# A gated linear attention with a feed-forward layer on one core: work by head and sequence, or by slabs of 128 tokens and 8 heads

## The chip, the core and the metric

The kernel runs on one core of a Trainium2 chip. A core has TensorE (PE, matrix products into PSUM; its weight loads are the row PEld), VectorE (DVE), ScalarE (ACT, functions from tables that are loaded as sets), GpSimd (POOL) and SyncE (SP, which here only issues DMAs); 16 DMA engines move data between DRAM and on-chip memory. Each engine works through its own list of instructions in order, and waits at an instruction until what it needs is there. The metric is the time of one execution on the device, in microseconds (us).

## The reference

The first stage is a linear attention with a complex gate for every token and channel: a state S of 48 x 48 for each of 4 x 8 heads is multiplied by the gate, takes up k v, and is read by q, over 768 tokens. The second is a gated feed-forward layer over all 3072 tokens.

```python
# B, H, S, D = 4, 8, 768, 48; d_model 384, d_ff 1536
mag = np.sqrt(a_re * a_re + a_im * a_im)
scale = np.minimum(mag, 0.999) / (mag + 1e-06)
a_re_n, a_im_n = (a_re * scale, a_im * scale)
for t in range(S):
    new_re = ar * S_re - ai * S_im
    new_im = ar * S_im + ai * S_re
    kv = np.einsum('bhd,bhe->bhde', k[:, :, t], v[:, :, t])
    S_re, S_im = (new_re + kv, new_im)
    y[:, :, t] = np.einsum('bhd,bhde->bhe', q[:, :, t], S_re)
x = y.transpose(0, 2, 1, 3).reshape(B * S, H * D)
gate = 1.0 / (1.0 + np.exp(-(x @ w_gate)))
out = gate * (x @ w_val) @ w_out
```

## The kernel before

The sequence is cut into 6 chunks of 128 tokens. A product of gates is a sum of log magnitudes and a sum of phases, and inside a chunk both sums are one product with a triangular matrix: `cl_ps` (L183) for the logs, `ct_ps` (L196) for the phases, both fp32. With exp of half the log sum and sine and cosine of the phase sum, q and k become rotated vectors `qst` and `kst`, 112 wide per head: 48 cosine parts, 16 zeros, 48 sine parts. Inside a chunk, attention is then k-transposed-q scores times a triangular mask, times v.

The outer loop runs over the 4 batches. `emit_prep(b)` loads q, k, v, a_re and a_im of one batch, head by head, as 128 x 288 tiles (128 tokens of each of 6 chunks), squares the gate (L149, L151), clips it (L153), divides im by re through a reciprocal (L159, L160), and takes Ln (L163) and Arctan (L165). The batch's loop then makes, for every head, `ee` = exp (L185, L186), the phase wrap (L200 to L206: round on ScalarE, subtract, then fold for the cosine on VectorE), sine and cosine (L209, L211) and the rotated vectors (L227 to L233).

Because sums are taken within a chunk and centred, going from chunk to chunk multiplies the state by a complex number per channel. Rows of `ee` and `cs` go to DRAM (`scr`) and back as columns (`rbe`, `rbc`, `rbn`), from which `alr` and `ngi` are formed (L245 to L264); the state's real part lies on partitions 0 to 47 and its imaginary part on 64 to 111, and L308 to L335 update it with operations on 48 partitions.

The chunk loop works by pairs of heads: four transposes (L282, L283) of the rotated vectors, one copy `qkT` (L286), two score products (L288), one mask (L290), then per head the output `py` (L297, L300), which has 48 rows and 128 token columns, its eviction `xall` (L302), and the state's new part `pkv` (L304). DMAs copy `xall` into `xt`, whose 128-partition tiles cross head borders. `emit_moe` then does 384 tokens at a time: 12 blocks of gate `pg` (L102), value `pv` (L107), tanh (L112) and product `p` (L114), and three output blocks `po` (L120). It uses two PSUM buffers. The order on each engine is set by a scheduler from the program order; POOL issues the loads of v and of the weights, SP all other DMAs.

## Time and profile before

| | us |
|---|---|
| median of 3 runs (624.09 to 624.98) | 624.13 |
| span of the profiled execution | 622.0 |
| DVE busy | 418.3 |
| PE busy | 384.9 |
| ACT busy | 304.7 |
| POOL busy | 275.5 |

Busy time is the sum of an engine's instructions; PE's are pipelined, so that neighbours overlap, and their starts tell more than their durations. In a table of windows each row is a stretch of the execution, its length, the busy time and number of instructions of PE, PEld, DVE, ACT and POOL in that order, then the granted TensorE clock as a share of the full one, the DMA engines' busy share and GB/s. In a row of groups stand line, engine, operation, tiles and shapes, count, then total and mean busy time (ns), then the idle time just ahead and who ended it. A row of waits is: engine, tile and line, who was waited for, us in total, times, and the longest. A row of the timeline is start, duration, engine, line and operation, with idle time in brackets.

### The profile page before, as it was taken

What the parts mean: (1) busy time and instruction counts of PE and PEld (TensorE: products, weight loads), DVE (VectorE), ACT (ScalarE), POOL (GpSimd) and SP (SyncE); (2) the same over time, 40 slices, a digit from 0 to 9 for tenths busy, and PEclk for the clock granted to TensorE, in tenths of its full rate; (3) what the DMA queues carried; (4) which work ended last, traced back from release to release, by engine and by line L of the source; (5) the groups of instructions that cost most, each with busy time, mean ns of one, the idle gap of its engine ahead of it and who ended that gap; (6) DMA issues with size and microseconds to landing.
All of it is one profiled execution on the core that took longest, in us unless ns stands there. A gap on an engine that the chain in (4) does not pass through costs nothing. (4 is left out here: it accounts for less than half of the span.)

```text
span 622.0 us, 7049 instructions
## 1 busy us (share of the span) xinstructions
PE 384.9 (62%) x2112; PEld 214.0 (34%) x2112; DVE 418.3 (67%) x757; ACT 304.7 (49%) x611; POOL 275.5 (44%) x358
## 2 busy tenths in 40 slices
PE   0011234349673327878665567989556988989897
PEld 0000112125441113544332234555233555444443
DVE  0374368987669898766769988577484987433432
ACT  0027957964145586322877973335856232322321
POOL 4449565648377656735536325555441333000000
PEclk9999999999555555755879559658796995899999
DMA  8999133452647154303614301004410010110011
GB/s 168 187 181 124 29 50 41 63 99 41 104 41 75 20 95 77 59 0 33 54 21 88 56 2 39 1 1 46 33 26 15 1 40 1 38 40 26 13 39 38
DMA packets 163270, 32.76 MB, mean 53 GB/s; under 512 B 155936, under 2 KB 162464, under 8 KB 163232
## 3 DMA queue, kind: packets, MB, share of 16 engines
q1 hardware_dynamic: 135552, 26.42, 24.2%
q0 software_dynamic: 27680, 5.90, 10.5%
q8 instruction: 16, 0.26, 0.2%
q14 instruction: 22, 0.18, 0.1%
HBM read 31.01 MB, written 4.83 MB: 58 GB/s over the span
## 5 line engine op out<-in xcount | busy, mean ns | idle before, releaser
L302 ACT ACTIVATE xall<-py 48x128 f16<-48x128 f32 x192 | 51.5, 268 | 132.4 <-PE py L300 112.1
L107 PE MATMUL pv<-xt,wv 128*128 128x384 f16 x288 | 73.9, 362 | 29.3 <-DVE p L114 26.4
L102 PE MATMUL pg<-xt,wg 128*128 128x384 f16 x288 | 76.1, 368 | 22.2 <-ACT g L112 18.9
L114 DVE SCALAR_TENSOR_TENSOR p<-g,pv 128x384 f16<-128x384 f16 x96 | 52.6, 548 | 54.0 <-PE pv L107 48.7
L112 ACT ACTIVATE g<-pg 128x384 f16<-128x384 f32 x96 | 47.0, 490 | 78.8 <-PE pg L102 78.1
L183 PE MATMUL cl_ps<-lm,wl_t 128*128 128x288 f32 x64 | 35.8, 678 | 78.0 <-ACT lm L163 40.4
L159 DVE RECIPROCAL th<-a 128x288 f32<-128x288 f32 x32 | 61.5, 1935 | 29.5 <-DMA a<-in_a_re_dram 25.5
L297 PE MATMUL py<-mst,v 128*48 128x128 f16 x192 | 51.7, 269 | 13.5 <-ACT xall L302 6.8
L290 DVE TENSOR_TENSOR mst<-cps,msk_t 128x256 f16<-128x256 f32 x96 | 40.4, 422 | 28.9 <-PE cps L288 26.8
L191 POOL TENSOR_TENSOR qke<-qke,ee 128x576 f32<-128x576 f32 x32 | 46.4, 1461 | 21.1 <-ACT ee L186 19.0
L304 PE MATMUL pkv<-v,kst 128*112 128x48 f16 x192 | 23.9, 246 | 50.0 <-POOL kst L231 50.0
L282 PE MATMUL cps<-idn_t,qst 128*112 128x128 f16 x192 | 49.7, 300 | 3.9 <-DVE mst L290 2.9
L120 PE MATMUL po<-wo,p 128*128 128x384 f16 x288 | 49.2, 330 | 3.3 <-ACT g L112 2.0
L288 PE MATMUL cps<-qkT 112*128 112x128 f16 x192 | 34.6, 276 | 25.2 <-DVE qkT L286 25.1
L107 PEld LDWEIGHTS <-wv 128*128 128x128 f16 x288 | 29.1, 107 | 58.6 <-issue 48.2
L283 PE MATMUL cps<-idn_t,kst 128*112 128x128 f16 x192 | 47.4, 286 | 2.3 <-POOL kst L231 1.4
L286 DVE COPY qkT<-cps 112x512 f16<-112x512 f16 x96 | 39.8, 418 | 13.3 <-PE py L300 10.4
L233 POOL TENSOR_TENSOR kst<-qke,cs 128x288 f16<-128x288 f32 x32 | 31.4, 981 | 36.4 <-ACT cs L209 36.3
L102 PEld LDWEIGHTS <-wg 128*128 128x128 f16 x288 | 30.0, 107 | 46.6 <-issue 32.9
L183 PEld LDWEIGHTS cl_ps<-lm,wl_t 128*128 128x128 f32 x64 | 16.3, 299 | 84.7 <-ACT lm L163 40.8
L300 PE MATMUL py<-qkT,x 112*48 112x128 f16 x160 | 44.0, 275 | 0.0
L151 POOL TENSOR_TENSOR lm<-sq 128x288 f32<-128x288 f32 x32 | 28.1, 883 | 31.5 <-DVE sq L149 31.4
(67 smaller groups left out, 866.5 us busy)
## 6 DMA issues: line engine op xcount, KB each, us to landing
a<-in_a_re_dram SPq DMA_DIRECT2D x32, 144.0 KB
a<-in_a_im_dram SPq DMA_DIRECT2D x32, 144.0 KB
qke<-in_q_dram SPq DMA_DIRECT2D x32, 144.0 KB
qke<-in_k_dram SPq DMA_DIRECT2D x32, 144.0 KB
out_dram<-ot SPq DMA_DIRECT2D x24, 192.0 KB
v<-in_v_dram POOLq DMA_DIRECT2D x32, 72.0 KB, 3.5
xt<-xall SPq DMA_DIRECT2D x24, 72.0 KB
wg<-in_moe_w_gate_dram POOLq DMA_DIRECT2D x3, 384.0 KB, 8.3
```

Of the source, the lines that this page charges most:

```text
L102: nc.tensor.matmul(pg, wg16[:, j, fc:fc + 128], xt[j][:, tok0:tok0 + ntok], start=(j == 0), stop=(j == 2))
L107: nc.tensor.matmul(pv, wv16[:, j, fc:fc + 128], xt[j][:, tok0:tok0 + ntok], start=(j == 0), stop=(j == 2))
L112: nc.scalar.activation(out=g16, in_=pg, func=FT.Tanh, scale=0.5)
L114: nc.vector.scalar_tensor_tensor(out=p, in0=g16, scalar=1.0, op0=ALU.add, in1=pv, op1=ALU.mult)
L120: nc.tensor.matmul(po, p16[fb][:, s0:s0 + 128], wo16[:, fb], start=(fb == 0), stop=(fb == NFB - 1))
L159: nc.vector.reciprocal(out=th, in_=a2[:, 0])
L183: nc.tensor.matmul(cl_ps, wl_t, lm, start=True, stop=True)
L191: nc.gpsimd.tensor_tensor(out=qke, in0=qke, in1=ee, op=ALU.mult)
L282: nc.tensor.transpose(pqkt[:, hh * 2], qst_h[h][:, c], idn_t)
L283: nc.tensor.transpose(pqkt[:, hh * 2 + 1], kst_h[h][:, c], idn_t)
L297: nc.tensor.matmul(py, v16_h[h][:, c], mst[:, hh], start=True, stop=(c == 0))
L302: nc.scalar.activation(out=xall[:, h, col0:col0 + L], in_=py, func=FT.Copy, scale=1.0 / YSC)
```

## The change

The work is cut anew into 24 slabs, each 128 tokens of one batch by all 8 heads (128 x 384), in 8 groups of three slabs.

- **Phase over the whole sequence.** `run` holds the sum of all phases of earlier slabs; a second fp32 product with a matrix of ones (`on_t`, L210) adds it to the triangular sum in the same PSUM tile. From slab to slab the state is then only multiplied by a real number, `arr` (L188); the complex parts, `rbc`, `rbn`, `alr` and `ngi` are gone. The decay row still goes to DRAM and comes back as a column (L181, L184), for both halves of the partitions.
- **Wrap on TensorE.** VectorE rounds the phase sum to `r16` (L221); a product with the negated identity (L223) takes it off in PSUM, sine reads it there (L226); L229 marks what is above a quarter, a second such product (L231) takes one off, and L233 reads the cosine with a bias of a quarter turn.
- **Log and angle.** a_re passes Ln and Exp to give the reciprocal; the log magnitude is 2 Ln(re) + Ln(1 + (im/re)^2), clipped in the log.
- **128-wide weights.** Rotated vectors are padded to 128 per head, in five pairs of fixed buffers whose zeros are written once. Transposes, scores and masks go by four heads (L284 to L300). The output `y` has tokens on its rows: its weights are `mst` and `qkT` (128 columns), v and state are the moving side (48 columns). One eviction and three transposes per slab give `xt` without DMAs.
- **Order.** The parts are generators that `merge` interleaves in program order: phase A is the attention of group g with the out projection of g-1 and the first half of the prep of g+1; phase B is gate and value of g with the second half of that prep. On ScalarE this order is kept as written, with table loads named; the other engines are still ordered by the scheduler. There are four PSUM buffers for the feed-forward and four for all else. The weight loads stand on POOL behind the first prep's last POOL operation, and v comes through SP as fp32 and is cast on POOL.

The diff, cut to its core:

```diff
-            sq = pas.tile([L, 2, CD], F32, name="sq", tag="sq")
-            nc.vector.tensor_tensor(out=sq, in0=a2, in1=a2, op=ALU.mult)
-            lm = pmid.tile([L, CD], F32, name="lm", tag="lm")
-            nc.gpsimd.tensor_tensor(out=lm, in0=sq[:, 0], in1=sq[:, 1],
-                                    op=ALU.add)
...
-            rr = pas.tile([L, CD], F32, name="rr", tag="rr")
-            nc.scalar.activation(out=rr, in_=ct_ps, func=FT.Copy, bias=RCONST)
...
-                nc.vector.tensor_tensor(out=u1[0:48], in0=tt[0:48], in1=ar_lo,
-                                        op=ALU.mult)
-                nc.gpsimd.tensor_tensor(out=u2[0:48], in0=tt[64:112],
-                                        in1=ai_hi, op=ALU.mult)
-                nc.vector.tensor_tensor(out=xst[0:48], in0=u1[0:48],
-                                        in1=u2[0:48], op=ALU.add)
...
+        nc.scalar.preload_act_table_set("natural_log_exp_and_others")
+        nc.scalar.activation(out=ar, in_=ar, func=FT.Ln)
+        nc.scalar.activation(out=inv, in_=ar, func=FT.Exp, scale=-1.0)
+        yield
+        for s in range(NS):
+            G.last_pool = nc.gpsimd.tensor_tensor(
+                out=ai[:, s], in0=ai[:, s], in1=inv[:, s], op=ALU.mult)
+            nc.scalar.activation(out=inv[:, s], in_=ai[:, s], func=FT.Square)
+            nc.scalar.activation(out=inv[:, s], in_=inv[:, s], func=FT.Ln,
+                                 bias=1.0)
...
+            cl = ps_gen.tile([L, HD], F32, name=f"cl_{g}_{s}", tag="gen")
+            nc.tensor.matmul(cl, wl_t, ar[:, s], start=True, stop=True)
+            nc.scalar.activation(out=G.ee[:, 0, s], in_=cl, func=FT.Exp,
+                                 scale=0.5)
...
+            nc.sync.dma_start(scr[b][c:c + 1], G.ee[L - 1:L, 0, s])
+            with nc.allow_non_contiguous_dma(reason="column of decays"):
+                for p0 in (0, 64):
+                    nc.sync.dma_start(
+                        rbe[b][p0:p0 + D, c],
+                        scr[b][c].rearrange("(h d) -> d h", d=D))
+            if c > 0:
+                nc.vector.tensor_tensor(
+                    out=arr[b][:, c - 1], in0=rbe[b][:, c - 1],
+                    in1=rbe[b][:, c], op=ALU.mult)
...
+            nc.tensor.matmul(ct, wt_t, th[:, s], start=True, stop=False,
+                             skip_group_check=True)
+            if c > 0:
+                nc.tensor.matmul(ct, on_t, run[b], start=False, stop=False,
+                                 skip_group_check=True)
...
+            r16 = psm.tile([L, HD], F16, name=f"r16_{g}_{s}", tag="r16")
+            nc.vector.tensor_scalar(out=r16, in0=ct, scalar1=RCONST,
+                                    scalar2=-RCONST, op0=ALU.add, op1=ALU.add)
+            nc.tensor.matmul(ct, nid_t, r16, start=False, stop=False,
+                             skip_group_check=True)
+            cs = pcs.tile([L, 2, HD], F32, name=f"cs_{g}_{s}", tag="cs")
+            nc.scalar.activation(out=cs[:, 1], in_=ct, func=FT.Sin,
+                                 scale=TWO_PI)
+            r2 = psm.tile([L, HD], F16, name=f"r2_{g}_{s}", tag="r2")
+            nc.vector.tensor_scalar(out=r2, in0=ct, scalar1=0.25,
+                                    scalar2=None, op0=ALU.is_gt)
+            nc.tensor.matmul(ct, nid_t, r2, start=False, stop=True,
+                             skip_group_check=True)
+            nc.scalar.activation(out=cs[:, 0], in_=ct, func=FT.Sin,
+                                 scale=TWO_PI, bias=pio2)
...
+            qs, ks = slots[(g * NS + s) % NSLOT]
+            for i, dst in enumerate((qs, ks)):
+                nc.vector.tensor_tensor(
+                    out=dst.rearrange("p h (r x) -> p h r x", r=2)[:, :, :, 0:D],
+                    in0=G.qk[:, i, s].rearrange("p (h d) -> p h d", d=D)
+                    .unsqueeze(2).broadcast_to([L, H, 2, D]),
+                    in1=cs.rearrange("p r (h d) -> p h r d", d=D),
+                    op=ALU.mult)
...
+                nc.vector.tensor_tensor(
+                    out=u, in0=P[b],
+                    in1=arr[b][:, c - 1].unsqueeze(2).broadcast_to([L, H, D]),
+                    op=ALU.mult)
+                x16 = pst_.tile([L, H, D], F16, name=f"x16_{g}_{s}", tag="x16")
+                nc.vector.tensor_scalar(out=x16, in0=u, scalar1=YSC,
+                                        scalar2=None, op0=ALU.mult)
...
+                for h in range(H):
+                    nc.tensor.matmul(kv[:, h], ks[:, h], v16[:, h],
+                                     start=True, stop=True)
+                pn = pst_.tile([L, H, D], F32, name=f"P_{g}_{s}", tag="P")
+                if c > 0:
+                    nc.vector.tensor_tensor(out=pn, in0=u, in1=kv, op=ALU.add)
...
+                for i in range(4):
+                    h = hf * 4 + i
+                    nc.tensor.transpose(tp[:, i], qs[:, h], idn_t)
+                    nc.tensor.transpose(tp[:, 4 + i], ks[:, h], idn_t)
+                qkT = patt.tile([L, 8, L], F16, name=f"qkT_{g}_{s}_{hf}",
+                                tag="qkT")
+                nc.vector.tensor_copy(out=qkT, in_=tp)
...
+                    nc.tensor.matmul(sc[:, i], qkT[:, 4 + i], qkT[:, i],
+                                     start=True, stop=True)
...
+            y = ps_gen.tile([L, H, D], F32, name=f"y_{g}_{s}", tag="gen")
+            for h in range(H):
+                if c > 0:
+                    nc.tensor.matmul(y[:, h], qkTs[h // 4][:, h % 4],
+                                     x16[:, h], start=True, stop=False)
+                nc.tensor.matmul(y[:, h], msts[h // 4][:, h % 4], v16[:, h],
+                                 start=(c == 0), stop=True)
+            y16 = patt.tile([L, HD], F16, name=f"y16_{g}_{s}", tag="y16")
+            nc.scalar.activation(out=y16, in_=y.rearrange("p h d -> p (h d)"),
+                                 func=FT.Copy, scale=1.0 / YSC)
...
+            for j in range(3):
+                nc.tensor.transpose(xp[:, j], y16[:, j * L:(j + 1) * L], idn_t)
+            nc.vector.tensor_copy(out=G.xt[:, :, s * L:(s + 1) * L], in_=xp)
...
+    with tc.manual_schedule(engines={ACT}):
+        run_all(prep_a(0))
+        with tc.issue_after(gs[0].last_pool.ins):
+            load_weights()
+        run_all(prep_b(0))
+        for g in range(NG):
+            st = [(attn(g), 21)]
+            if g > 0:
+                st.append((outproj(g - 1), 9))
+            if g + 1 < NG:
+                loads_a(g + 1)
+                loads_q(g + 1)
+                st.append((prep_a(g + 1), 7))
+            merge(*st)
+            st = [(gateval(g), 12)]
+            if g + 1 < NG:
+                st.append((prep_b(g + 1), 4))
+            merge(*st)
+        run_all(outproj(NG - 1))
```

VectorE, before: a stretch of the third batch's preparation, in which gate products (`p`) alternate with the wrap of `ct_ps` and the rotation of q.

```order
L114 SCALAR_TENSOR_TENSOR p_5_2331<-g_0_5_2329,pv_5_2325 128x384
L227 TENSOR_TENSOR qst<-qke,cs 128x6x48
L229 TENSOR_TENSOR qst<-qke,cs 128x6x48
L227 TENSOR_TENSOR qst<-qke,cs 128x6x48
L114 SCALAR_TENSOR_TENSOR p_6_2343<-g_0_6_2341,pv_6_2337 128x384
L201 SCALAR_TENSOR_TENSOR ffc<-rr,ct_ps 128x288 x2
L114 SCALAR_TENSOR_TENSOR p_7_2355<-g_0_7_2353,pv_7_2349 128x384
L204 TENSOR_SCALAR ffc<-ffc 128x288
```

VectorE now, in phase B of group 2, from its third gate product on (`r` is the rounded phase and then the quarter mark, `rbe` the decays that came back from DRAM):

```order
L338 SCALAR_TENSOR_TENSOR p_1596<-g_2_2_1627,pv_2_1623 128x384
L188 TENSOR_TENSOR arr_160<-rbe_158 128x8
L221 TENSOR_SCALAR r_3_0_1671<-ct_0_1666 128x384
L188 TENSOR_TENSOR arr_160<-rbe_158 128x8
L338 SCALAR_TENSOR_TENSOR p_1596<-g_2_3_1641,pv_3_1637 128x384
L338 SCALAR_TENSOR_TENSOR p_1596<-g_2_4_1652,pv_4_1648 128x384
L338 SCALAR_TENSOR_TENSOR p_1596<-g_2_5_1663,pv_5_1659 128x384
L229 TENSOR_SCALAR r_3_0_1676<-ct_0_1666 128x384
L237 TENSOR_TENSOR qst_148<-qk_1272,cs_0_1674 128x16x48
L237 TENSOR_TENSOR kst_149<-qk_1272,cs_0_1674 128x16x48
```

The two decay products now stand between gate products, and the two rotations of a slab, each for all heads, stand between two runs of three gate products.

VectorE now, in phase A of group 2, at the border of its slabs 1 and 2:

```order
L300 TENSOR_TENSOR mst_1_0_1425<-sc_1_0_1420,msk_t 128x512
L300 TENSOR_TENSOR mst_1_1_1436<-sc_1_1_1431,msk_t 128x512
L167 SCALAR_TENSOR_TENSOR a_3_1265<-a_3_1265,inv_1323 128x384
L259 TENSOR_TENSOR u_2_1474<-P_1_1386,arr_160 128x384
L170 TENSOR_SCALAR a_3_1265<-a_3_1265 128x384
L264 TENSOR_SCALAR x_2_2_1476<-u_2_1474 128x384
L320 COPY xt_1284<-xp_1_1462 128x3x128
L273 TENSOR_TENSOR P_2_1487<-u_2_1474,kv_2_1478 128x384
L288 COPY qkT_2_0_1509<-tp_2_0_1500 128x1024
L288 COPY qkT_2_1_1525<-tp_2_1_1516 128x1024
```

Between the last mask of one slab and the first copy of the next stand the state, a step of the next group's prep, and the copy of the finished slab's transposes.

GpSimd now, at the start, from the third weight load of the gate on (ahead of it stand the three divisions of the first prep, four weight loads, and slab 0's scaling and cast):

```order
L139 DMA wg_152<-in_moe_w_gate_dram 128x1536
L191 TENSOR_TENSOR qk_118<-qk_118,ee_192 128x2x384
L140 DMA wv_153<-in_moe_w_val_dram 128x1536
L193 CAST v_0_120<-v_0_119 128x384
L142 DMA wo_154<-in_moe_w_out_dram 128x384 x3
L191 TENSOR_TENSOR qk_118<-qk_118,ee_192 128x2x384
L142 DMA wo_154<-in_moe_w_out_dram 128x384
L193 CAST v_0_120<-v_0_119 128x384
L142 DMA wo_154<-in_moe_w_out_dram 128x384 x8
L217 TENSOR_TENSOR run_1_259<-a_0_99 128x384
```

The first running sum of phases, which slab 2 needs, stands behind all weight loads.

491 lines of the change are left out of this document (212 added, 279 removed).

## The prediction

> **What bounds the kernel now.** I read the page's first two lines, then the window table by stage, then the table of waits and the groups by shape. All sums below are made against the profiled execution's span of 622.0 us; the median of the runs, 624.13 us, is 2.1 us above it, and I add those 2.1 us at the end.
>
> ```profile
> span 622.0 us, 7049 instructions
> PE 384.9 (62%) x2112; PEld 214.0 (34%) x2112; DVE 418.3 (67%) x757; ACT 304.7 (49%) x611; POOL 275.5 (44%) x358
> ```
> ```profile
> 0.00:50.00 50.00, 2.59 (x5) 1.39 (x6) 21.15 (x21) 8.52 (x13) 23.26 (x39) 1.00 1.28 178
> ...
> 100.00:550.00 450.00, 306.12 (x1739) 171.75 (x1738) 346.73 (x650) 242.20 (x505) 219.52 (x272) 0.74 0.29 42
> ...
> 550.00:622.00 72.00, 60.63 (x338) 32.55 (x336) 26.06 (x47) 17.64 (x36) 0.00 (x0) 0.99 0.09 32
> ```
>
> No engine is full. Between 100 and 550 us VectorE (DVE) is busy for 346.73 of 450 us, 77%; the first 50 us are loading, and the last 72 us are feed-forward alone on TensorE (PE).
>
> ```profile
> ACT xall L302 <- PE py L300: 112.1, 129, 7.3
> ...
> PEld L304 <- POOL kst L231: 58.4, 19, 10.1
> ...
> ACT lm L163 <- DVE lm L153: 48.9, 10, 37.9
> ...
> PE pv L107 <- DVE p L114: 26.4, 50, 3.1
> ```
>
> The waits form a ring: ACT on PE, PE on POOL and DVE, DVE on loads. So VectorE's work, spread at 77%, sets the middle, and latency sets the two ends. I take the new kernel as startup, eight groups, tail.
>
> **VectorE's work after, per group of three slabs.**
>
> ```profile
> L159 DVE RECIPROCAL th<-a 128x288 f32<-128x288 f32 x32 | 61.5, 1935 | 29.5 <-DMA a<-in_a_re_dram 25.5 <-PE ct_ps L196 3.9
> L114 DVE SCALAR_TENSOR_TENSOR p<-g,pv 128x384 f16<-128x384 f16 x96 | 52.6, 548 | 54.0 <-PE pv L107 48.7 <-ACT g L112 4.5 <-ACT xall L302 0.4
> ...
> L290 DVE TENSOR_TENSOR mst<-cps,msk_t 128x256 f16<-128x256 f32 x96 | 40.4, 422 | 28.9 <-PE cps L288 26.8 <-PE py L297 0.2
> L286 DVE COPY qkT<-cps 112x512 f16<-112x512 f16 x96 | 39.8, 418 | 13.3 <-PE py L300 10.4 <-PE cps L283 2.3
> ...
> L149 DVE TENSOR_TENSOR sq<-a 128x576 f32<-128x576 f32 x32 | 29.9, 942 | 2.0 <-DMA a<-in_a_im_dram 2.0
> ...
> L229 DVE TENSOR_TENSOR qst<-qke,cs 128x288 f16<-128x288 f32 x32 | 25.4, 795 | 4.3 <-ACT cs L209 4.3
> ...
> L206 DVE SCALAR_TENSOR_TENSOR ffc<-ffc 128x288 f32<-128x288 f32 x32 | 18.8, 603 | 0.0
> ...
> L319 DVE TENSOR_TENSOR u<-tt,alr 48x384 f32<-48x384 f32 x20 | 15.2, 758 | 0.3
> ...
> L123 DVE TENSOR_SCALAR ot<-po 128x384 f32<-128x384 f32 x24 | 13.2, 551 | 16.5 <-PE po L120 16.5
> ```
>
> The reciprocal (61.5 us) goes to ScalarE as Ln and Exp; the 48-partition state updates become 128-partition ones. What is left per group, in us:
> - gate products 12 x 0.548 = 6.6.
> - Rotated q and k, 6 of 768 elements. L319 and L149 (384 and 576 elements, both inputs in SBUF) give 0.96 ns per element, so 1.13 each; the ends are 0.94 (L149, fewer elements) and 2.1 (L229's rate of 2.76 ns per element). I take 1.13, the rate of the two wide rows: 6.8.
> - qkT copies, 6 of 1024 (ends 0.42 and 0.84 from L286, taken 0.70): 4.2.
> - Masks, 6 of 512: L290 and L123 give 1.0 ns per further element, 0.68 each: 4.1.
> - The two rounding steps that feed the wrap, 6 x 0.55 as L123: 3.3.
> - In the first half of a slab's prep, 3 x 0.70 (L206 stretched to 384) and 3 x 0.5: 3.6.
> - State: 2.5 x (0.76 + 0.5 + 0.55) = 4.5. The xt copies 3 x 0.42 = 1.25, the decay products 0.5.
>
> Sum 34.8 us, 279 us in all against 418.3. About 17.6 of it stand in phase A (attention of a group, with the out projection of the last and the first half of the next prep), 17.2 in phase B (gate and value products, with the second half of the next prep).
>
> **TensorE after.** The next rows are its timeline at both clocks.
>
> ```profile
> 124.37 0.31 PE L282 MATMUL cps<-idn_t,qst 128*112 128x128 f16 x1
> 124.47 0.31 PE L283 MATMUL cps<-idn_t,kst 128*112 128x128 f16 x1
> ```
> ```profile
> 40.44 2.29 PE L183 MATMUL cl_ps<-lm,wl_t 128*128 128x288 f32 x4 [40.44 <-ACT lm L163]
> ...
> 510.87 0.22 PE L282 MATMUL cps<-idn_t,qst 128*112 128x128 f16 x1
> 510.93 0.22 PE L283 MATMUL cps<-idn_t,kst 128*112 128x128 f16 x1
> ...
> 511.42 0.59 PE L304 MATMUL pkv<-v,kst 128*112 128x48 f16 x8
> ...
> 516.15 0.31 PE L283 MATMUL cps<-idn_t,kst 128*112 128x128 f16 x1
> 516.26 0.31 PE L282 MATMUL cps<-idn_t,qst 128*112 128x128 f16 x1
> ...
> 522.84 0.94 PE L304 MATMUL pkv<-v,kst 128*112 128x48 f16 x8
> ```
> ```profile
> 568.49 5.86 PE po L120 x36
> ```
>
> A 128-column pair starts every 0.056 us at full clock and every 0.107 at half; a 48-column one 0.074 and 0.117; a 384-column one 0.163. An fp32 product of 288 columns took 1.15 us, and pairs of that early stretch start 0.10 us apart, half clock, so one of 384 is 1.53, or 0.76 at full. Per group at full clock: feed-forward 108 x 0.163 = 17.6; fp32 sums 8.5 x 0.76 = 6.5 (the running phase sum adds 2.5 of them); the wrap by the negated identity 6 x 0.163 = 1.0; attention 3 x (27 x 0.056 + 24 x 0.074) = 9.9. Sum 35.0, phase A 18, phase B 17. PE and DVE are now level. The weight loads of 128 columns instead of 112 I cost at nothing: the pairs above start at the pace of their moving columns. If that cover is gone, in the 48-column products, it is inside the 0.074.
>
> **ScalarE and GpSimd.**
>
> ```profile
> L112 ACT ACTIVATE g<-pg 128x384 f16<-128x384 f32 x96 | 47.0, 490 | 78.8 <-PE pg L102 78.1 <-DVE qkT L286 0.5
> ...
> L163 ACT ACT_TABLE_LOAD x23 | 29.5, 1283 | 1.1 <-PEq L376 0.7
> ...
> L151 POOL TENSOR_TENSOR lm<-sq 128x288 f32<-128x288 f32 x32 | 28.1, 883 | 31.5 <-DVE sq L149 31.4
> ```
>
> ACT: 36 of 384 elements at 0.49 to 0.55, 3 of 1152 at 1.2, 4 table loads of 1.283: some 27 us per group. POOL at 883 ns for 288 elements: eight of 384 to 768 and three casts, 13 us. The cast stands in no row; between 0 and the 1.18 that L151's rate gives a two-input operation it stays hidden, since POOL is idle two thirds of a group (taken 0.8). The row scatters and the copies of xt between partitions go from the DMA queues, which the 100 to 550 us row shows busy 0.29 of the time: nothing. Both engines lie beside PE and DVE except at the places below.
>
> **Phase A: 25 us.** In slab 0 the out projection (36 x 0.163) and attention (3.3) fill PE: 9.2. Slabs 1 and 2 stand one behind the other on PE and DVE. DVE has 17.6/3 = 5.9 per slab. Behind the second mask come eight y pairs, y16 on ACT, three transposes, an fp32 sum, the next eight transposes, with three hand-overs of 0.36 (the row at 525.64 below): at half clock 0.94 + 0.49 + 0.32 + 1.53 + 0.86 + 1.1 = 5.2, of which DVE fills 3.4 with state and prep. So 5.9 + 1.8, with the first qkT copy 8; at full clock it is 6.
>
> ```profile
> 525.64 0.26 PE L297 MATMUL py<-mst,v 128*48 128x128 f16 x1 [0.36 <-ACT xall L302]
> ...
> 528.59 0.39 PE L288 MATMUL cps<-qkT 112*128 112x128 f16 x2 [0.97 <-DVE qkT L286]
> ```
>
> These rows lie in a stretch of pure attention with pairs at 0.107 us, though PE never rested longer than about 1 us. The slabs are used no more densely, so I take half clock there: 9.2 + 8 + 8 = 25.
>
> **Phase B: 20.7 us.** PE needs 11.7 + 4.2 + 1.0 = 16.9. Added: behind the third gate ACT does two table loads and the arctan of 1152 elements, 3.7 us, while four PSUM buffers let PE run two blocks (1.96) ahead: 1.8. Each pair of rotations holds the gate products 2.3 us against that lead: 1.0 for three. The decay column: a row goes to DRAM and comes back, and its product stands on DVE ahead of the fourth gate product. Queued behind it are the whole of phase B's DVE work and so PE. Nearest landing:
>
> ```profile
> v<-in_v_dram POOLq DMA_DIRECT2D x32, 72.0 KB, 3.5
> ```
>
> Two of 3.5 make 7 us, with about 6 us of cover: 1.0 (0 to 7). Sum 20.7; a group is 45.7. Check by the middle of before: 34.8 us of DVE at 77% are 45.2.
>
> **Startup: 63 us.**
>
> ```profile
> 1.26 0.74 POOL L89 DMA_DIRECT2D wg<-in_moe_w_gate_dram  x1 [0.80 <-POOLq L376]
> ...
> 11.58 4.49 SPq L143 DMA_DIRECT2D qke<-in_k_dram  x1
> ...
> 17.68 1.95 DVE L159 RECIPROCAL th<-a 128x288 f32<-128x288 f32 x1 [16.36 <-DMA a<-in_a_re_dram]
> ...
> 19.25 1.17 POOL L92 DMA_DIRECT2D wo<-in_moe_w_out_dram  x2 [0.21 <-issue]
> ```
> ```profile
> q1 hardware_dynamic: 135552, 26.42, 24.2%
> ```
>
> 24.2% of 622 us for 26.42 MB is 5.7 us per MB. The six loads of a (1.18 MB) now go first, with the weights held back: they land at about 10 us instead of 17.68. Three slabs of prep then take ACT and POOL some 1.1 us each per step: sums and Exp end at 21, arctan and tables at 24. Slabs 0 and 1 are rotated by 31. But POOL's first running sum stands behind eighteen weight issues, which took 1.26 to 20.4 us before; started at 15 with 8 us of POOL's own work between, they end near 39. Slab 2's phase waits for that sum, and in ACT's order y16 of slab 0 stands behind slab 2's sines and behind the next group's Ln, whose loads share the DMA engines with the weights (an issue then took 4.49 us) and land at about 45. So y16 of slab 0 ends near 49, and two more slabs of 7 end attention at 63.
>
> **Sum.** 63 + seven B of 20.7 (144.9) + a last B without prep (12.5) + six A of 25 (150) + a last A without prep (21) + tail (36 x 0.163 + 0.5 + 3.5 = 9.9) = 401.3, with 2.1 outside the span **403 us**.
>
> **Rivals.**
> - Full clock in the slabs: six A of 21 and a last of 19 give 403 - 26 = 377. For it: slab 0 is dense. Against it: the stretch at 525 us. The Trainium skill, "TensorE: Matmul & The Clock Gate", section "HAM oscillation — how this bites in real kernels", states that idle gaps under about 3.4 us keep the clock up; by that rule this rival holds. The stretch at 525 us, half clock with gaps of 0.36 to 0.97 us, speaks against the rule.
> - Phases overlap to the bound of PE or DVE, 35 us per group: besides the clock, B falls to 17.5, 7 x 3.2 = 22 less: 355. Each engine's order is fixed, and that speaks against it.
> - The orders fit the chip badly, and DVE reaches only the 67% it has over the whole span: 34.8/0.67 = 52 per group, 7 x 6.3 more: 447.
> - PE at half clock in B too: 17 us more in each B, A at 33: 403 + 8 x 14 + 7 x 8 = 570. The tail's 0.163 at a granted 0.99 speaks against it.
> - Slower than before: SP issues in order, and each slab's decay row must land before SP can issue the next loads. At the worst rows, 4.49 for an issue and 3.5 for a landing, a trip is 16 us against a cover of 5; 21 slabs x 11 = 231 more, 634. It decides from 10.5 us per slab. Against it: DMA is busy 0.29 of its time in the middle.
>
> **How the numbers follow.** 403 (its own range 375 to 430) 0.45; full clock 0.20; overlap 0.10; bad fit 0.17; half clock 0.05; SP 0.03. From 345 to 475 leaves out under 0.1 by the cases; the unknown rotations (0.94 to 2.1 us, up to +47 in all) are the reason to keep the upper end. A measurement of this kernel can tell about 0.2% from no change. Faster 0.96, same 0.01, slower 0.03.
>
> **What would show it.** Rotations near 1.1 us, qkT near 0.7, masks near 0.68; a group every 45 us, read from the starts of successive gate blocks; first y16 near 49 us; granted clock near 0.5 in slabs 1 and 2 and near 1 in B; DVE busy near 280 us. Wrong would be: PE waiting long for the table loads, DVE long on the decay product, or a startup far from 63.

## The result and the profile after

The changed kernel takes **383.48 us** (median of 4 runs, 381.77 to 384.09); the kernel before took 624.56 us beside it (4 runs, 624.09 to 626.13). The ratio is 0.613, 95% interval 0.6108 to 0.6151. The forecast was 403 us with a range of 345 to 475: the time lies in the range, and also in the narrower one of the likeliest case, 375 to 430, but 19.5 us under the number itself. Where one execution of an experiment stands apart from its others (e8: 385.84 us against 377.76 to 380.52; e9: 677.27 against 375.71 to 377.29; e11: 378.6 against 372.14 to 376.25), the ratio is of the others and the median of all, and as it is the profiled one in all three, only their times and granted clocks are used.

First the page of the kernel after: its span, and busy time, share and instructions of each engine.

```profile
span 382.3 us, 6035 instructions
...
PE 291.6 (76%) x2208; PEld 179.5 (47%) x2208; DVE 244.3 (64%) x451; ACT 199.8 (52%) x343; POOL 107.1 (28%) x114
```

VectorE fell from 418.3 to 244.3 us, TensorE from 384.9 to 291.6, and TensorE is now the busiest. The forecast had put VectorE at the level of TensorE; it stands well below. Next the groups of the kernel after by shape: busy time, mean ns of one, idle time before them and what ended it.

```profile
L338 DVE SCALAR_TENSOR_TENSOR p<-g,pv 128x384 f16<-128x384 f16 x96 | 49.4, 549 | 21.1 <-ACT g L337 17.6 <-PE pv L334 3.4
L237 DVE TENSOR_TENSOR qst<-qk,cs 128x768 f16<-128x768 f32 x24 | 23.0, 958 | 12.3 <-ACT cs L233 10.6 <-ACT g L337 1.0 <-issue 0.6
L288 DVE COPY qkT<-tp 128x1024 f16<-128x1024 f16 x48 | 32.3, 684 | 13.9 <-PE tp L285 13.7
L300 DVE TENSOR_TENSOR mst<-sc,msk_t 128x512 f16<-128x512 f32 x48 | 31.4, 681 | 3.3 <-PE sc L296 3.2
```

Gate products (0.549 us), qkT copies (0.684) and masks (0.681) came as forecast from rows of the kernel before; a rotation takes 0.958 us and not 1.13.

The stretches of a group are marked by the function table that ScalarE loads: the one of the gates (line 337) opens phase B, the one of Ln (line 157) opens phase A. Here are a B and an A from the window table of the kernel after: stretch and length, then busy time with instruction count of PE, PEld, DVE, ACT and POOL, the granted clock, the DMA share and GB/s. Below it is the stretch from the first y16 to the first B.

```profile
152.57:175.03 22.46, 20.90 (x131) 12.28 (x129) 16.36 (x30) 13.35 (x22) 4.00 (x4) 1.00 0.52 81
175.03:196.19 21.16, 15.28 (x151) 10.12 (x149) 14.13 (x26) 11.65 (x21) 7.80 (x8) 0.84 0.40 85
```
```profile
49.00:67.20 18.20, 12.81 (x118) 9.50 (x119) 12.05 (x24) 7.84 (x17) 8.21 (x8) 0.63 0.71 109
```

In B TensorE is busy for 20.90 of 22.46 us at full clock, with hardly a pause. In A no engine is full. The transposes in the timeline below start 0.06 or 0.10 us apart, at the full pace or about half of it, and a granted clock of 0.84 on average means half clock for 2 x 0.16 x 21.16 = 6.8 us. Between the first y16 and the first B it is 2 x 0.37 x 18.2 = 13.5 us.

Now TensorE's timeline of the kernel after, from the last two slabs of one group to the first slab of the next: start, duration, operation, and in brackets the idle time before it with what ended it.

```profile
179.13 0.34 PE L319 MATMUL xp<-idn_t,y 128*128 128x128 f16 x3 [0.26 <-ACT y L314]
179.31 0.36 PE L269 MATMUL kv<-v,kst 128*128 128x48 f16 x8
179.51 0.22 PE L284 MATMUL tp<-idn_t,qst 128*128 128x128 f16 x1
179.57 0.22 PE L285 MATMUL tp<-idn_t,kst 128*128 128x128 f16 x1
...
180.34 0.22 PE L285 MATMUL tp<-idn_t,kst 128*128 128x128 f16 x1
...
182.85 0.40 PE L296 MATMUL sc<-qkT 128*128 128x128 f16 x4 [2.28 <-DVE qkT L288]
184.18 0.40 PE L296 MATMUL sc<-qkT 128*128 128x128 f16 x4 [0.94 <-DVE qkT L288]
...
186.69 0.50 PE L319 MATMUL xp<-idn_t,y 128*128 128x128 f16 x3 [0.58 <-ACT y L314]
...
188.38 0.31 PE L284 MATMUL tp<-idn_t,qst 128*128 128x128 f16 x1
188.48 0.31 PE L285 MATMUL tp<-idn_t,kst 128*128 128x128 f16 x1
```
```profile
194.22 0.34 PE L319 MATMUL xp<-idn_t,y 128*128 128x128 f16 x3 [0.58 <-ACT y L314]
...
198.03 0.65 PE L330 MATMUL pg<-xt,wg 128*128 128x384 f16 x3 [0.81 <-ACT g L337]
...
201.78 1.53 PE L207 MATMUL ct<-a,wt_t 128*128 128x384 f32 x4 [0.66 <-issue]
...
216.17 0.32 PE L231 MATMUL ct<-r,nid_t 128*128 128x384 f16 x1 [0.22 <-DVE r L229]
...
221.75 0.34 PE L319 MATMUL xp<-idn_t,y 128*128 128x128 f16 x3
```

The three xp rows at 179.13, 186.69 and 194.22 stand at the end of slabs 0, 1 and 2: slabs 1 and 2 take 7.56 and 7.53 us. From 194.22 to the next group's 221.75 are 27.53 us, and the three brackets in it (0.81, 0.66, 0.22) are all that TensorE rests there. The other groups are alike: 27.2 to 28.5 us there, and 7.0 to 7.6 us for each of the two slabs. The window table of the kernel after has the two slabs apart:

```profile
179.13:186.69 7.56, 3.08 (x51) 2.36 (x51) 6.51 (x13) 3.84 (x9) 2.65 (x3) 0.92 0.78 153
186.69:194.22 7.53, 6.39 (x47) 4.39 (x47) 3.41 (x7) 2.61 (x7) 2.83 (x2) 0.63 0.09 29
```

So a group is some 27.5 us in which TensorE is full, and two slabs of equal length that differ in kind. In slab 1 the clock is nearly full (0.92), TensorE is busy for 3.08 of 7.56 us and waits for VectorE. In slab 2 TensorE is busy for 6.39 of 7.53 us, most of it at half clock (0.63): the two transposes at 179.51 start 0.06 us apart, the two at 188.38 0.10 us.

### The profile page after: what moved, and what is told of

The parts are those of the page before. It is cut to its first block, busy times and chain, and to the rows that moved or that the text cites. A ratio compares the mean times of both kernels' runs of the same rounds, so it can differ in the third digit from the quotient of the medians.

```text
span 382.3 us, 6035 instructions
## 1 busy us (share of the span) xinstructions
PE 291.6 (76%) x2208; PEld 179.5 (47%) x2208; DVE 244.3 (64%) x451; ACT 199.8 (52%) x343; POOL 107.1 (28%) x114
## 4 chain that ended last, share of the span: by engine, by line
issue 33%; PE 26%; DVE 12%; ACT 9%; POOL 7%; DMA 6%; SPq 5%; POOLq 0%; ACTq 0%
PE cl L176 6%; DMA qk<-in_k_dram 5%; DVE mst L300 4%; PE pg L330 4%; DVE a L167 3%; PE po L347 3%; PE pv L334 3%; POOL run L217 3%; SPq L109 3%; DVE qkT L288 2%; ACT y L314 2%; POOL a L162 2%; PE xp L319 2%; PE tp L285 2%; PE tp L284 2%
## 5 line engine op out<-in xcount | busy, mean ns | idle before, releaser
L191 POOL TENSOR_TENSOR qk<-qk,ee 128x768 f32<-128x768 f32 x24 | 43.9, 1829 | 74.4 <-ACT ee L179 45.2
L338 DVE SCALAR_TENSOR_TENSOR p<-g,pv 128x384 f16<-128x384 f16 x96 | 49.4, 549 | 21.1 <-ACT g L337 17.6
L162 POOL TENSOR_TENSOR a<-a,inv 128x384 f32<-128x384 f32 x24 | 24.8, 1060 | 114.3 <-ACT inv L159 114.3
L337 ACT ACTIVATE g<-pg 128x384 f16<-128x384 f32 x96 | 43.9, 489 | 21.7 <-PE pg L330 21.6
L288 DVE COPY qkT<-tp 128x1024 f16<-128x1024 f16 x48 | 32.3, 684 | 13.9 <-PE tp L285 13.7
L176 PE MATMUL cl<-a,wl_t 128*128 128x384 f32 x48 | 29.8, 724 | 14.3 <-DVE a L170 14.3
L296 PE MATMUL sc<-qkT 128*128 128x128 f16 x192 | 21.9, 245 | 22.1 <-DVE qkT L288 21.9
L221 DVE TENSOR_SCALAR r<-ct 128x384 f16<-128x384 f32 x24 | 13.3, 554 | 33.3 <-PE ct L210 17.8
L233 ACT ACTIVATE cs<-ct,pio 128x384 f32<-128x384 f32 x24 | 14.0, 581 | 38.9 <-PE ct L231 38.9
L300 DVE TENSOR_TENSOR mst<-sc,msk_t 128x512 f16<-128x512 f32 x48 | 31.4, 681 | 3.3 <-PE sc L296 3.2
L347 PEld LDWEIGHTS <-p 128*128 128x128 f16 x288 | 25.9, 97 | 14.6 <-issue 1.1
L284 PE MATMUL tp<-idn_t,qst 128*128 128x128 f16 x192 | 32.7, 250 | 0.0
L285 PE MATMUL tp<-idn_t,kst 128*128 128x128 f16 x192 | 32.3, 250 | 0.0
L237 DVE TENSOR_TENSOR qst<-qk,cs 128x768 f16<-128x768 f32 x24 | 23.0, 958 | 12.3 <-ACT cs L233 10.6
```

The costliest lines, as they stand in the source:

```text
L176: nc.tensor.matmul(cl, wl_t, ar[:, s], start=True, stop=True)
L191: nc.gpsimd.tensor_tensor(out=G.qk[:, :, s], in0=G.qk[:, :, s], in1=G.ee[:, :, s], op=ALU.mult)
L284: nc.tensor.transpose(tp[:, i], qs[:, h], idn_t)
L285: nc.tensor.transpose(tp[:, 4 + i], ks[:, h], idn_t)
L288: nc.vector.tensor_copy(out=qkT, in_=tp)
L296: nc.tensor.matmul(sc[:, i], qkT[:, 4 + i], qkT[:, i], start=True, stop=True)
```

## The experiments

Each ratio is against the kernel before on the same chip; the kernel after stands at 0.613 (0.6108 to 0.6151). In the diffs, minus is the kernel after.

**e1: 112 columns again.**

```
-  nc.tensor.transpose(tp[:, i], qs[:, h], idn_t)
+  nc.tensor.transpose(tp[0:W, i], qs[:, h, 0:W], idn_t)
...
-  nc.tensor.matmul(kv[:, h], ks[:, h], v16[:, h],
+  nc.tensor.matmul(kv[0:W, h], ks[:, h, 0:W], v16[:, h],
```

> Only the padded width is undone: transposes, scores and the state's new part use 112 of the 128 columns or partitions, so that their weight loads are 112 wide again. In the changed kernel 48-column products start every 0.025 us at full clock where 112-wide ones took 0.074 before. Theory W (the width pays through the weight loads): the eight state products of a slab return to 0.074, +0.4 us a slab at full clock, most of it ahead of the next slab's transposes; 20 slabs with such products and the 112-wide transposes give 5 to 10 us more, 389 to 394 us. Rival (loads are hidden behind the moving columns, as I costed them): within 2 us of 383.5.

Measured: 383.42 us, ratio 0.6127 (0.6111 to 0.6143): no difference, as the rival has it. The padding nevertheless does something on TensorE. First two groups of e1 by shape, then the same two of the kernel after.

```profile
L270 PE MATMUL kv<-v,kst 128*112 128x48 f16 x160 | 13.6, 223 | 2.6 <-DVE kst L238 2.6
...
L270 PEld LDWEIGHTS <-kst 128*112 128x112 f16 x160 | 13.0, 156 | 4.7 <-DVE kst L238 3.3
```
```profile
L269 PE MATMUL kv<-v,kst 128*128 128x48 f16 x160 | 8.7, 192 | 2.6 <-DVE kst L237 2.6
...
L269 PEld LDWEIGHTS <-kst 128*128 128x128 f16 x160 | 7.6, 104 | 5.1 <-DVE kst L237 3.5
```

On average a load of 128 columns takes 104 ns and one of 112 columns 156 ns; the products of 48 columns keep TensorE busy for 8.7 instead of 13.6 us. The Trainium skill, "TensorE: Matmul & The Clock Gate", section "Weight-path perf modes — Fast Weight Load (FWL) and DoubleRow", states when the fast load is on: when the number of weights is 128 and their type is not fp32. The rows agree (a factor of 1.5 here). The total doesn't show the 4.9 us saved; the likely reason, not tested, is that they lie in slabs whose length something else sets.

**e2: one after the other instead of merged.**

```
-            merge(*st)
+            run_all(attn(g))
+            if g > 0:
+                run_all(outproj(g - 1))
+            if g + 1 < NG:
+                run_all(prep_a(g + 1))
+            run_all(gateval(g))
+            if g + 1 < NG:
+                run_all(prep_b(g + 1))
```

> Only the program order is undone: attention, out projection, first half of the next prep, gate and value, second half of the next prep, one behind the other, on ScalarE as written. Theory M (the merge carries the gain, because ScalarE's list is fixed): the out projection (6 us), the prep's first half (7) and second half (9) no longer lie beside attention and gate blocks: up to 12 us more in each of 7 groups, 440 to 470 us. Rival (the scheduler of the other engines pulls the work together anyway): within 10 us of 383.5.

Measured: 486.35 us, ratio 0.7772 (0.7751 to 0.7792), 103 us slower, more than either expectation has. The page of e2:

```profile
span 485.6 us, 6076 instructions
...
PE 348.3 (72%) x2208; PEld 206.0 (42%) x2208; DVE 248.0 (51%) x451; ACT 203.6 (42%) x343; POOL 105.4 (22%) x114
```

VectorE's work is the same (248.0 against 244.3), TensorE's same 2208 products take 57 us longer. The granted clock is 0.758 over the span, so half clock for some 2 x 0.242 x 485.6 = 235 us, against 75 us in the kernel after (0.902). So the merge is worth 103 us, and part of that is the clock: with attention and feed-forward apart, TensorE rests more and spends three times as long at half clock.

**e3: the phase wrap on VectorE.** The two subtractions, which were products with the negated identity, go to VectorE, where the rounding and the comparison already were.

```
-            nc.tensor.matmul(ct, nid_t, r16, start=False, stop=False,
+            nc.vector.tensor_tensor(out=ff, in0=ct, in1=rr, op=ALU.subtract)
...
-            nc.tensor.matmul(ct, nid_t, r2, start=False, stop=True,
+            nc.vector.tensor_tensor(out=fc, in0=ff, in1=fc, op=ALU.subtract)
```

> Only the phase wrap goes back to VectorE: rounding, subtraction, mark and second subtraction there (about 2.0 us per slab in place of 1.1), and no product with the negated identity. Theory V (VectorE's sum sets phase B): +0.9 us x 24 slabs, 22 us more, 400 to 408 us. Rival (in phase B the hand-overs between TensorE, VectorE and ScalarE set it; sine waited 26 us in all for the first product and 39 us for the second): fewer hand-overs, 370 to 384 us.

Measured: 385.48 us, ratio 0.6168 (0.6146 to 0.6189). The intervals overlap; the wrap on TensorE is worth 2 us or nothing, and neither expectation comes. VectorE's busy time rises to 259.5 us and TensorE's falls to 281.4, and neither moves the time: 15 us more on the one and 10 less on the other. Theory V's loss doesn't come: VectorE has room. That TensorE's 10 us bring no gain either suggests that its full timeline in B is not the only bound there (behind the rounding, VectorE now does three steps in a row ahead of the second sine). Which offsets the other wasn't taken apart.

**e4: two PSUM buffers instead of four for the feed-forward.**

```
-    ps_moe = pool("ps_moe", 4, **PSUM)
+    ps_moe = pool("ps_moe", 2, **PSUM)
```

> Two PSUM buffers for the feed-forward instead of four. Theory P (the lead of two blocks carries phase B over the table loads and the rotations): a block falls back to the 1.36 us that it took before, 12 x 0.39 us in each of 8 groups, and the table loads stop TensorE for 3.7 us instead of 1.8: 40 to 50 us more, 420 to 435 us. Rival (ScalarE and VectorE set the pace of B): under 10 us more.

Measured: 406.83 us, ratio 0.65 (0.6485 to 0.6514), 23 us slower, between the two expectations. The gate and value products of e4, then of the kernel after, with the idle time before them at the end:

```profile
L334 PE MATMUL pv<-xt,wv 128*128 128x384 f16 x288 | 65.6, 336 | 12.7 <-ACT g L337 7.4 <-DVE p L338 4.8
L330 PE MATMUL pg<-xt,wg 128*128 128x384 f16 x288 | 64.9, 335 | 15.5 <-ACT g L337 13.7 <-DVE p L338 0.7 <-DVE xt L320 0.4
```
```profile
L330 PE MATMUL pg<-xt,wg 128*128 128x384 f16 x288 | 64.5, 329 | 7.5 <-ACT g L337 5.7 <-DVE p L338 0.6 <-DVE xt L320 0.4
L334 PE MATMUL pv<-xt,wv 128*128 128x384 f16 x288 | 63.2, 329 | 0.0
```

TensorE rests 28.2 us ahead of them instead of 7.5. The 20.7 us between are nearly the whole loss: four buffers hide most of the table loads and rotations behind TensorE, and with two they stand in the open.

**e5: the weights later.** The gate and value weights are loaded only once the first group's running sums stand on GpSimd (POOL), the output weights behind the next group's divisions.

```
-        with tc.issue_after(gs[0].last_pool.ins):
-            load_weights()
         run_all(prep_b(0))
+        with tc.issue_after(gs[0].last_run.ins):
+            load_weights()
...
+            if g == 0:
+                with tc.issue_after(gs[1].last_pool.ins):
+                    load_wo()
```

> Gate and value weights are loaded behind the first group's running phase sums instead of ahead of them, the out projection's weights behind the second group's divisions. Theory S (the startup waits for POOL's list and for q and k of slab 2, which the weights hold up: the last load of group 0 was issued for 12.4 us and k of slab 2 landed at 33 us): slab 2's sines move from 44 to about 31 us, the first y16 from 50 to about 36, and the first feed-forward table load from 67.2 to 52 to 56 us; 370 to 374 us in all. Rival (the DMA engines are 0.95 busy up to 67 us, so the same bytes take the same time and gate weights or group 1 arrive late instead): within 3 us of 383.5.

Measured: 376.32 us, ratio 0.6025 (0.6 to 0.6049): 7 us faster than the kernel after, between the two expectations. POOL's timeline of the kernel after, then of e5:

```profile
33.07 1.80 POOL L191 TENSOR_TENSOR qk<-qk,ee 128x768 f32<-128x768 f32 x1 [8.98 <-DMA qk<-in_k_dram]
...
35.86 4.23 POOL L142 DMA_DIRECT2D wo<-in_moe_w_out_dram  x8
40.05 1.06 POOL L217 TENSOR_TENSOR run<-a 128x384 f32<-128x384 f32 x1
```
```profile
22.03 0.99 POOL L219 TENSOR_TENSOR run<-a 128x384 f32<-128x384 f32 x1 [0.64 <-ACT a L202]
```

And ScalarE's timeline of e5:

```profile
41.40 1.16 ACT L160 ACTIVATE a<-a 128x1152 f32<-128x1152 f32 x1 [4.17 <-DMA a<-in_a_re_dram]
...
43.66 0.47 ACT L317 ACTIVATE y<-y 128x384 f16<-128x384 f32 x1
...
61.47 1.28 ACT L340 ACT_TABLE_LOAD   x1
```

In the kernel after a k load held POOL for 8.98 us, and eight weight issues stood ahead of the running sum; in e5 neither does, and the sum stands at 22.03. Which of the two counts for more isn't parted. The first y16 comes 6.2 us earlier (43.66 against 49.85), and the first B at 61.47 instead of 67.19. The 18 us by which the sum comes earlier do not all arrive, since y16 now stands behind the next group's Ln on ScalarE (41.40), which waits for its loads.

**e6: one table load less per group.** The table that holds arctan is loaded ahead of the gates, so that Tanh and arctan share it (24 loads instead of 31).

```
+        if g + 1 < NG:
+            nc.scalar.preload_act_table_set("sigmoid_and_others")
         G.p = pp.tile([128, NFB, NT], F16,
```

> The set that holds both tanh and arctan is loaded ahead of the gate blocks, so that the separate load ahead of the arctan goes: 3 table loads per group instead of 4. Theory T (ScalarE's stop behind the third gate is on the path of phase B): 7 x 1.28 us less, 374 to 377 us. Rival (TensorE's lead or the phase chain behind it covers the load): within 2 us of 383.5.

Measured: 380.32 us, ratio 0.608 (0.606 to 0.6101): about 3 us less than the kernel after; the intervals just miss each other (0.6101 and 0.6108). Seven loads of 1.283 us are 9.0 us of ScalarE, and a third of that arrives, less than theory T has and more than its rival.

**e7: the decay product later in VectorE's order.**

```
-            if c > 0:
-                nc.vector.tensor_tensor(
-                    out=arr[b][:, c - 1], in0=rbe[b][:, c - 1],
...
+                nc.vector.tensor_tensor(
+                    out=arr[b][:, c - 1], in0=rbe[b][:, c - 1],
                 u = pst_.tile
```

> The product of two decay columns moves from the prep to the place where the state uses it, so that VectorE no longer waits for the DRAM round trip among the gate products (9.5 us of waits in 8 places in the changed kernel). Theory D (that wait is on the path): 3 to 9 us less. Rival (it lies beside ScalarE's table loads, and the scheduler may put it elsewhere): within 2 us of 383.5.

Measured: 383.8 us, ratio 0.6133 (0.6115 to 0.6151): nothing, as the rival has it. The row of the kernel after, then of e7:

```profile
L188 DVE TENSOR_TENSOR arr<-rbe 128x8 f32<-128x8 f32 x20 | 4.5, 224 | 9.6 <-DMA rbe<-scr 9.5
```
```profile
L254 DVE TENSOR_TENSOR arr<-rbe 128x8 f32<-128x8 f32 x20 | 4.1, 209 | 5.4 <-DMA rbe<-scr 5.3
```

The wait for the row that comes back from DRAM shrinks from 9.5 to 5.3 us, and the total doesn't notice. What is left of that wait, 5.3 us in all, wasn't tested.

**e8: every transpose into tp twice.** 384 products more, which compute the same again.

```
+                    for _ in range(2):
-                    nc.tensor.transpose(tp[:, i], qs[:, h], idn_t)
+                        nc.tensor.transpose(tp[:, i], qs[:, h], idn_t)
```

> Every transpose of rotated q and k is done twice, 16 more products of 128 columns per slab: 0.9 us at full clock, 1.7 at half. Theory C (density sets the granted clock: slabs 1 and 2 rest at half clock for some 7 us per group because TensorE is too thinly used): the half-clock stretch shrinks, and the time grows by less than 24 x 0.9 = 21 us, perhaps not at all: 383 to 395 us. Rival (TensorE's work in the slab is simply on the path): 21 to 35 us more, 405 to 418 us.

Measured: 380.17 us, ratio 0.6065 (0.6042 to 0.6087). More work for TensorE, and no more time, as theory C has it; the rival's 21 us don't come. Its four runs lie 8 us apart (377.76 to 385.84), so a gain of 3 us isn't shown. The granted clock of the four is 0.920 to 0.950, against 0.888 to 0.906 in the runs of the kernel after. So half clock goes with too little work on TensorE, and the added products pay for themselves with the clock.

**e9: no running phase sum.** Left out is the sum over the earlier slabs of a sequence (POOL's running sum and the product with the ones matrix).

```
-            if c > 0:
-                nc.tensor.matmul(ct, on_t, run[b], start=False, stop=False,
-                                 skip_group_check=True)
-            if c < NCH - 1:
+            if False:
```

> Leaves out the sum of the phases of the slabs ahead of a slab (the product with the ones matrix and the running sum on POOL), so every slab is computed as if it stood at the start of its sequence. Theory P: TensorE sets the length of stretch B (in the after profile it is busy 19.1 of 20.9 us there, at full clock). Two float32 records of the ones product stand 0.64 us apart from the next instruction at 203.15 to 203.79, and 21 slabs have the product, 2.6 per group: B gets 1.7 us shorter, 11.6 in seven, and the startup 0.6 to 1.9 (the startup's chain has POOL run 1.03 and PE ct L210 1.66): 370 to 372 us. Rival R: the round trips through rounding and sines set B, TensorE only fills in: 382 to 384, B's length as before and the startup 1 to 2 us shorter.

Measured: 376.84 us, ratio 0.6027 (0.6013 to 0.6041), 6.5 us under the kernel after: between the two. How much of it is the startup (where e5 gains 7 us by letting the same sum come earlier) and how much phase B stays open. Of the 24 slabs 20 have the product left out, not 21 as the expectation says. So the whole-sequence sum, startup included, costs some 6.5 us.

**e12: half of the qkT copies on ScalarE.**

```
-                nc.vector.tensor_copy(out=qkT, in_=tp)
+                if hf == 0:
+                    nc.vector.tensor_copy(out=qkT, in_=tp)
+                else:
+                    nc.scalar.activation(out=qkT, in_=tp, func=FT.Copy)
```

> Moves the second of a slab's two qkT copies from VectorE to ScalarE. Theory Q: in stretch A TensorE waits for these copies (21.9 us of idle time in all ahead of the score products) and what is slow is VectorE's row of steps (14.1 to 16.4 of 21 us busy there): with 24 copies of 0.684 us off VectorE and the two of a slab side by side, each slab's chain loses up to 0.7 us, 24 x 0.5 to 0.7 = 12 to 16 us in all: 367 to 372. Rival S: ScalarE takes the copy in its turn, behind sines, gates and evictions of y, and its copy of 1024 columns takes about 1 us (the 384-column eviction of y takes 0.47): the gain is lost again, 380 to 390.

Measured: 384.64 us, ratio 0.6158 (0.6141 to 0.6175): no gain. The same two stretches of e12, and the new copy's group:

```profile
152.43:175.80 23.37, 21.80 (x135) 12.58 (x132) 17.17 (x31) 14.25 (x24) 3.97 (x4) 1.00 0.50 77
175.80:196.16 20.36, 14.42 (x144) 9.69 (x145) 11.54 (x23) 13.58 (x24) 7.65 (x8) 0.83 0.43 88
```
```profile
L291 ACT ACTIVATE qkT<-tp 128x1024 f16<-128x1024 f16 x24 | 24.4, 1015 | 7.9 <-PE tp L285 7.9
```

A is 0.8 us shorter (20.36 against 21.16), as theory Q has it, and B 0.9 longer (23.37 against 22.46), as rival S has it; by the table loads that mark them it is so in all six groups. ScalarE's copy takes 1.015 us against 0.684.

**e10 and e11: together.** e10 is e5 and e6; e11 adds e8.

> The late weight loads and the shared function table together. Theory: they act in different places (startup; ScalarE at the ends of A and B), so their gains of 7 and 3 us add: 373 to 374. Rival: the table load that was saved was saved at a place where the other now decides: 376 as with the late weights alone.

> The same two, and every transpose into tp done twice. Theory C: TensorE has room in A, its clock falls because too little is on it, and more work there keeps the clock up: 3 us under the two edits alone, 370 to 371, and less than 70 us at half clock in the records. Rival: the doubled products only fill idle time, the difference to the two edits alone is under 1 us, to either side; with TensorE as A's bound it would be slower by 24 x 16 x 0.056 = 21 us.

Measured: e10 376.55 us, ratio 0.6034 (0.6014 to 0.6055); e11 375.9 us, ratio 0.6001 (0.5977 to 0.6026). The gain of e6 doesn't add to that of e5, as e10's rival has it. The 3 us that theory C expects of e11 under e10 don't come either: 0.65 us lie within the intervals, though the granted clock is 0.941 to 0.954 against 0.886 to 0.909 in e10. e11 has the lowest median, but its interval overlaps those of e5 and e10: the largest gain of one edit that computes the same is e5's, 1.7%, and nothing here adds to it measurably.

## Why the prediction was right, and where it was off

By its own terms, in the profiled execution: the startup up to the first B 67.2 us against 63; the six groups after it (first B to seventh, 67.19 to 323.30 in ScalarE's table loads) 42.7 us each against 45.7; the end from there to the span's end 59.0 against 20.7 + 21 + 12.5 + 9.9 = 64.1. So +4.2, -18.1 and -5.1 make 382.3 of 401.3. What is left of the 19.5 us, half a microsecond, lies outside the span and in rounding. The way in which the parts add up was right; several of the parts came out near for other reasons than the forecast's, and those are named below.

**Startup: the right wait, its length in part by luck, and 4 us short.** The first y16, and the gates' first and seventh table load, from ScalarE's timeline of the kernel after:

```profile
49.85 0.47 ACT L314 ACTIVATE y<-y 128x384 f16<-128x384 f32 x1
...
67.19 1.28 ACT L337 ACT_TABLE_LOAD   x1
...
323.30 1.28 ACT L337 ACT_TABLE_LOAD   x1
```

The first y16 was forecast near 49 and stands at 49.85. The running sum behind the weight issues was to end near 39; it ended at 41.1, and e5, which takes it out of there, shows that this order was worth 6 us. But the time ahead of the sum is made up otherwise than forecast: the eighteen issues, which stand behind the divisions of the first prep and among its scalings, were counted at 19.1 us and took 10.0 (6.4 + 1.9 + 1.7 in the groups of POOL), and the wait of 8.98 us for k of slab 2, which the term didn't have, filled the difference. The forecast's own numbers, 15 + 19.1 + 8, make 42 and not 39. What was short is the stretch behind the first y16, 14 us forecast and 17.3 measured: two slabs of 7.6 and 7.2 instead of 7, and 2 us from the end of the last y16 (65.17) to the gates' table load, in which ScalarE waits 1.13 us for the last log sum of the next prep and takes its two exps; the term left them out.

**Group: waits in B too large.** The step on phase B added 1.8 us for table loads, 1.0 for rotations and 1.0 for the decay column to TensorE's 16.9. The timeline shows 1.7 us of waits from 194.22 to 221.75, and e4 shows why: four buffers cover most of the rest. Nearly halving the waits for the decay column gained nothing (e7). That is 2.1 us less per group. TensorE's work there, which nearly fills the stretch, came out right in sum: 27.53 - 1.7 = 25.8 us, against 16.9 + 9.2 forecast for B and slab 0. Two of its prices were too high, the 48-column products (next paragraph) and an fp32 product of 384 columns, 0.64 us by the starts in TensorE's timeline (203.15 to 203.79) against 0.76; what makes up for them wasn't taken apart. Where the boundary between the phases lies is a matter of the mark: slab 0's transposes already run in B, so that A reads 21.1 (25 forecast) and B 21.6 on average (20.7 forecast).

**Slabs 1 and 2: nearly right for reasons that were half wrong.** 7.55 us each were measured in this group, 8 forecast, 0.9 us less per group. The forecast took half clock for both; it lasts 6.8 us of the 15.1, and 5.6 of them lie in slab 2 (2 x 0.37 x 7.53). The products of 48 columns were taken at 0.074 us apart and stand 0.025 apart in kv (179.31 to 179.51, eight of them). Nearly half of that is a misreading: the row of 0.59 us for eight holds the last product's own duration too, and by their single starts they stood 0.052 apart at full clock in the kernel before. The rest is the width: e1's 112 columns bring back 0.052, so the step that costs the weights of 128 columns at nothing should have read that they gain. The chain behind the second mask also prices sixteen y products as eight (0.94 us at half clock). Against all this stands what the term hadn't, a wait: the next group's prep stands ahead of qkT on VectorE and waits for ScalarE.

```profile
181.00 1.19 DVE L167 SCALAR_TENSOR_TENSOR a<-a,inv 128x384 f32<-128x384 f32 x1 [0.67 <-ACT inv L165]
182.11 0.68 DVE L288 COPY qkT<-tp 128x1024 f16<-128x1024 f16 x1
```

In VectorE's timeline of the kernel after, qkT starts at 182.11, though slab 1's last transpose began at 180.34: VectorE stands at a step of the prep, which itself waited for ScalarE. Another order of these two wasn't tried, so how much of slab 1 it costs isn't shown.

**The end: the last A was mis-sized.** Forecast were 21 us for an A without prep, which fits 9.2 for slab 0 and 5.9 for each of the others. ScalarE's timeline of the kernel after, the last sine and the last three y16:

```profile
345.16 0.58 ACT L233 ACTIVATE cs<-ct,pio 128x384 f32<-128x384 f32 x1 [2.58 <-PE ct L231]
...
349.32 0.49 ACT L314 ACTIVATE y<-y 128x384 f16<-128x384 f32 x1 [3.57 <-PE y L311]
...
353.89 0.49 ACT L314 ACTIVATE y<-y 128x384 f16<-128x384 f32 x1 [3.71 <-PE y L311]
...
358.19 0.49 ACT L314 ACTIVATE y<-y 128x384 f16<-128x384 f32 x1 [3.42 <-PE y L311]
```

Without prep, slabs follow at 4.57 and 4.30 us. Between the last sines of the phase B ahead (345.16 + 0.58 = 345.74) and the last y16 (358.68) are 12.9 us. Slab 0 takes 4.1 us of them (to 349.81), since 17 of the 36 products of the out projection already run in the B ahead, which takes 22.4 us (20.7 forecast). The last B takes 14.4 (12.5 forecast; the last gate ends at 373.07), the tail 9.2 (9.9).

The difference of some 3.1 us to the 7.5 of a slab with prep has two causes, which other traces part. Here is slab 1 of a group in e5, then slab 2 of one in e5 and of one in e4:

```profile
88.03:95.59 7.56, 3.66 (x52) 2.76 (x52) 6.51 (x13) 3.85 (x9) 3.42 (x4) 0.73 0.77 152
95.59:102.15 6.56, 5.19 (x47) 3.66 (x48) 3.30 (x7) 2.61 (x7) 3.27 (x3) 0.79 0.45 95
```
```profile
103.75:109.07 5.32, 3.85 (x48) 2.76 (x48) 3.33 (x7) 2.62 (x7) 2.77 (x2) 1.00 0.78 147
```

Slab 1 takes 7.56 us at a granted clock of 0.92 (kernel after) and at 0.73 (e5): its excess goes with the prep, not with the clock. Slab 2, with the same number of VectorE and ScalarE instructions, takes 7.53 us at 0.63 (kernel after), 6.56 at 0.79 (e5) and 5.32 at full clock (e4, which differs in the feed-forward's buffers alone): some 2.2 of its 3.2 us go with the clock. So the forecast's half clock is the right reason for one of the two slabs.

**VectorE's 279 us: 244.3.** The 279 us are a sum of durations, the 244.3 time busy. Count times mean over VectorE's groups of the kernel after makes 267 us, so 12 of the 35 us are prices: rotations were 0.17 us too dear (48 of them, 8 us), the states 0.578 + 0.605 + 0.549 instead of 0.76 + 0.5 + 0.55. The other 23 are overlap of neighbours: two masks in a row take 1.28 us, not 1.36. The check that set 34.8 us at 77% mixed the two as well, and its 45.2 us is no support for the length of a group, which VectorE doesn't fill.

**The rivals.** Two of them were partly true: full clock in the slabs (377 us) for more than half of their time, and the overlap (355 us) for the stretch in which TensorE is full. The measured time lies between these and the forecast. The rival with half clock in B, which is wrong, also names 17 us for each B and adds 14. The rule named beside the first (the Trainium skill, "TensorE: Matmul & The Clock Gate", section "HAM oscillation — how this bites in real kernels": "no PE-idle gaps >~3.4µs") isn't enough to keep the clock up in this kernel. Between 180.3 and 186.7 us the longest gap is 2.28 us, and the clock is at half by 188.4; from 67 us to the last A no gap of TensorE is longer than 2.29 us, and the clock falls to half in each of the six groups. What e8 shows instead is that the share of work counts: the same slabs with more products have a higher clock (0.92 to 0.95). e2's lower clock (0.758), with less work beside the attention, fits this, but TensorE also rests up to 4.45 us at a time there, so e2 alone wouldn't decide.

## What to carry to other kernels

Count the work of each engine by stage, then ask which waits the buffers already cover: here four accumulators hid most of ScalarE's table loads and VectorE's rotations, and taking two away cost 23 us. A sum or a load that stands behind bulk issues on one queue can set the startup; to move the issues behind it gave the largest gain of a later edit. In this kernel sparse work on TensorE cost twice, by its waits and by the clock (in e2 the same products took 57 us longer), so interleaving it with dense work was worth more than the idle time it fills.

## What was not expected of the hardware

- Products that only repeat others made the kernel no slower (e8: 0.6065 against 0.613; e11 against e10: 0.6001 and 0.6034), while the granted clock rose from about 0.90 to between 0.92 and 0.95.
- The granted clock fell to half for 6.8 us in each of six groups, though TensorE never rested longer than 2.29 us there.
- A weight load of 128 columns took 104 ns on average and one of 112 columns 156 ns; products of 48 columns follow each other at twice the pace with the wider load (0.025 against 0.052 us at full clock).
- ScalarE copies 1024 columns from PSUM in 1.015 us, VectorE in 0.684 us.
